# Reading exponentials from the SBUF copy, and joining two memory products in one PSUM bank, in a gated mix of two linear-attention branches

## The chip, the cores and the metric

The kernel runs on one core of one Trainium2 chip. The metric is the device time of the core in microseconds (us). Before the change it was 440.26 us, the median of six runs (439.39 to 441.11). PE is the TensorE matmul, PEld its weight load, DVE is VectorE, ACT is ScalarE, POOL is GpSimd.

## The reference, cut to what matters

Branch A is a "hedgehog" linear attention, branch B an attention in four segments with a memory carried from one segment to the next. A gate mixes their outputs. The change touches branch B alone:

```python
phi = lambda t: jnp.where(t > 0, t + 1.0, jnp.exp(t))
for s in range(4):                     # 4 segments of 512 rows; 32 heads of 20
    qs, ks, vs = q[:, :, s], k[:, :, s], v[:, :, s]
    p = _softmax(qs @ ks.T * scale + mask)
    a_dot = p @ vs
    pq = phi(qs)
    a_mem = (pq @ M) / (pq @ z + 1e-06)       # read the memory
    outs.append(g * a_mem + (1.0 - g) * a_dot)
    pk = phi(ks)
    M = M + pk.T @ vs                         # update the memory
    z = z + sum(pk)
```

## The kernel before

Branch B's loop runs over 32 groups: 4 segments times 8 groups of four heads. In each group PE makes the scores `st`, ACT turns them into `PT` by an exponential, POOL masks them, PE multiplies by the values into `nd`. Between these, PE is given "fill" work of other parts (projections of the next segment, branch A's queries, output matmuls). PE's order is fixed by hand; a scheduler orders the other engines' queues.

In this kernel every matmul writes into a tile in PSUM, from which DVE or ACT reads the result; all other tiles are in SBUF. A bank is the unit in which the kernel hands out PSUM, 512 fp32 columns on 128 partitions, and it uses eight of them. Four belong to `st` (two tiles of two banks). The other four, from the pool `psw`, are taken in turn by everything else, and that is what this case is about:

```python
psw = ctx.enter_context(tc.tile_pool(name="psw", bufs=4, space=PSUM))
ctx.enter_context(tc.manual_schedule(engines={mybir.EngineType.PE}))

def wtile(name, dt=F32):
    # ... (bf16 form cut)
    return psw.tile([P, 512], F32, name=name, tag="w")

def b_k(s, c):                                   # keys, 128 rows
    # ... (kp, pk, ek, rk: SBUF tiles)
    for hf in range(2):
        ps = wtile("kb_ps")
        mm_x(ps[:, 0:320], sc, WkB, 320 * hf, 320 * hf + 320)
        nc.vector.tensor_copy(out=kp[:, c, hf * 16:hf * 16 + 16, 0:DH],
                              in_=ps[:, 0:320].rearrange("p (h d) -> p h d", d=DH))
        if s < NSEG - 1:
            nc.scalar.activation(out=ek[:, hf * 320:hf * 320 + 320], in_=ps[:, 0:320],
                                 func=ACT.Exp)
    # ... (phi of k: rk = max(k, 0) + 1, then pk = min(rk, ek), both on DVE)

def b_q(s, g):                                   # queries of one group
    ps = wtile("qb_ps")
    # ... (five matmuls into ps)
    qT = bw.tile([P, L], BF16, name="qT", bufs=2)
    nc.vector.tensor_copy(out=qT, in_=ps)
    phiq = None
    if s > 0:
        eq = bw.tile([P, L], BF16, name="eq", bufs=1)
        nc.scalar.activation(out=eq, in_=ps, func=ACT.Exp)
        rq = bw.tile([P, L], BF16, name="rq")
        nc.vector.tensor_scalar(out=rq, in0=qT, scalar1=0.0, scalar2=1.0,
                                op0=ALU.max, op1=ALU.add)
        phiq = bw.tile([P, L], BF16, name="phiq", bufs=3)
        nc.vector.tensor_tensor(out=phiq, in0=rq, in1=eq, op=ALU.min)
    return qT, phiq

def b_mem(s, g, phiq):
    tm = None
    if s > 0:                                    # read the memory
        am = wtile("am_ps")
        for j in range(4):
            nc.tensor.matmul(am[:, j * 84:(j + 1) * 84], lhsT=phiq[:, j * P:(j + 1) * P],
                             rhs=Mbd[:, g].rearrange("p i e -> p (i e)"), start=True, stop=True)
        tm = b_norm(am, s, g, Cm, "m")           # DVE: rm = 1/den, rm *= Cm, tm = num * rm
    if s < NSEG - 1:                             # update the memory
        mz = wtile("mz_ps")
        # ... (four matmuls accumulate phi(k)^T v in mz[:, 0:84])
        # ... (DVE: Msb = mz + Msb, then Mbd = Msb * mask)
    return tm

for k in range(NG):                              # NG = 32
    # ...
    for t, cs in enumerate(((0,), (1, 3), (2,))):
        b_qk(qT, kT, PT, cs)                     # st, then PT
        if t == 0 and k + 1 < NG:
            nq = b_q(*divmod(k + 1, G))          # next group's queries
        if t == 1 and k + 1 < NG:
            nxt = (nq, b_kT(*divmod(k + 1, G)))
        if prev is not None:
            # ... t == 0: b_mem of the last group; t == 1, 2: b_pv of the last group into nd
        while fill and fill[0][0] < k + SHARE[t]:
            fill.pop(0)[1]()
```

The softmax here doesn't subtract the row's maximum and nothing guards it: scores larger than these inputs give would overflow.

## Time and profile before

| | before |
|---|---|
| device time, median | 440.26 us |
| span in the profile | 437.4 us |
| loop over the groups (101 to 412 us): PE, ACT, DVE busy | 258, 217, 185 of 311 us |
| PE waits on the q exponential `eq` | 9.6 us, 12 times |
| mean granted TensorE clock | 0.941 |

The first lines are of the page of the kernel before: busy time of each engine with its share of the span, and the chain of work that ended last, by engine. The line after them is the view by stretches for the loop (busy time and number of instructions of each engine, then granted clock, DMA share, GB/s).

```profile
PE 365.7 (84%) x4289; PEld 236.0 (54%) x4289; DVE 261.4 (60%) x680; ACT 274.8 (63%) x515; POOL 211.1 (48%) x365
...
PE 51%; ACT 19%; DVE 15%; POOL 9%; issue 4%; DMA 2%; POOLq 0%; SPq 0%; DVEq 0%; ACTq 0%
...
101.00:412.00 311.00, 257.88 (x3116) 153.83 (x3114) 185.40 (x539) 217.29 (x366) 141.76 (x251) 0.94 0.02 7
```

No engine is full. PE holds half of the chain, and the order of its matmuls is fixed (the same 4289 in the same order in the traces of before and of `qk_again`), so while one matmul waits for a bank PE stands. The view of waits for PE in the kernel before (who waited for whom: us in total, times, longest) shows for what:

```profile
PE st L428 <- ACT PT L434: 13.0, 25, 1.4
PE num_ps L518 <- DVE ts L538: 5.9, 3, 3.7
PE num_ps L518 <- ACT eq L401: 5.1, 5, 1.0
...
PE otp L551 <- ACT eq L401: 1.8, 2, 0.9
...
PE kb_ps L231 <- ACT eq L401: 1.0, 2, 0.5
...
PE kT_ps L412 <- ACT eq L401: 0.9, 2, 0.6
...
PE vb_ps L231 <- ACT eq L401: 0.8, 1, 0.8
```

Matmuls that have nothing to do with `eq` (branch A's `num_ps`, output transposes, next keys) wait for it, because they were given the bank that `eq` was still reading. One such wait, from the timeline of the kernel before (start, us, engine, instruction, in brackets the idle time before it and its releaser):

```profile
201.86 0.69 DVE L397 CAST qT<-qb_ps 128x512 bf16<-128x512 f32 x1 [1.33 <-PE qb_ps L393]
...
201.95 0.34 PE L518 MATMUL num_ps<-KVZ,Eq 128*128 128x132 bf16 x3
...
202.64 0.61 ACT L401 ACTIVATE eq<-qb_ps 128x512 bf16<-128x512 f32 x1
...
203.30 0.33 PE L518 MATMUL num_ps<-KVZ,Eq 128*128 128x132 bf16 x3 [1.01 <-ACT eq L401]
```

The DVE copy ends at 202.55, ACT's exponential of the same bank starts only then and ends at 203.25, and the second half of the `num_ps` matmuls waits 1.01 us for it.

Durations that the change rests on, from the groups by shape (count, busy us, mean ns, idle before):

```profile
L397 DVE CAST qT<-qb_ps 128x512 bf16<-128x512 f32 x32 | 22.1, 691 | 46.1 <-PE qb_ps L393 46.0
...
L401 ACT ACTIVATE eq<-qb_ps 128x512 bf16<-128x512 f32 x24 | 14.4, 602 | 4.9 <-DVE qT L397 2.7 <-DVE rq L403 1.5
...
L372 ACT ACTIVATE ek<-kb_ps 128x320 bf16<-128x320 f32 x24 | 10.3, 439 | 13.3 <-DVE kpad_150 L369 11.0 <-DVE kpad_156 L369 2.1
```

### The profile page before, as it was taken

The page shows a single profiled execution, that of the slowest core. Times are in us where ns is not written, and L with a number is a line of the kernel's source. Part 1 is how long each engine was busy: PE and PEld are TensorE (multiplying, and loading weights), DVE is VectorE, ACT ScalarE, POOL GpSimd, SP SyncE. Part 2 cuts the span into 40 slices and gives each one's busy share as a digit, 9 for nine tenths or more (in the row PEclk, how much of TensorE's full clock was granted, in tenths as well). Part 3 has the DMA queues.
Part 4 walks back from the last instruction along what each step waited for, and adds up shares of the span by engine and source line. Part 5 has one row for each costly group of instructions (what it writes and reads, how often), then busy time and mean ns, then how long its engine had stood idle before and what let it go on. Part 6 is the DMA issues. An engine that isn't in the chain of part 4 may idle for free.

```text
span 437.4 us, 10502 instructions
## 1 busy us (share of the span) xinstructions
PE 365.7 (84%) x4289; PEld 236.0 (54%) x4289; DVE 261.4 (60%) x680; ACT 274.8 (63%) x515; POOL 211.1 (48%) x365
## 2 busy tenths in 40 slices
PE   1999999797888687888988888898887788787686
PEld 1677877674444343455555555565554454445465
DVE  5378666787357453677665557665666556555431
ACT  1576666525887466676875777586675886765502
POOL 9037877860355434544453434554345555444520
PEclk9999999999999796899998999999999998988569
DMA  8960000000000000000000000000000000000001
GB/s 257 363 193 32 5 1 1 0 1 1 2 1 1 2 1 0 1 2 2 16 16 1 16 2 16 1 16 6 13 17 1 16 1 16 17 2 15 11 16 51
DMA packets 10610, 12.49 MB, mean 29 GB/s; under 512 B 1347, under 2 KB 10563, under 8 KB 10563
## 3 DMA queue, kind: packets, MB, share of 16 engines
q1 hardware_dynamic: 10563, 11.83, 8.2%
q8 instruction: 33, 0.54, 0.5%
q14 instruction: 14, 0.11, 0.1%
HBM read 9.21 MB, written 2.62 MB: 27 GB/s over the span
## 4 chain that ended last, share of the span: by engine, by line
PE 51%; ACT 19%; DVE 15%; POOL 9%; issue 4%; DMA 2%; POOLq 0%; SPq 0%; DVEq 0%; ACTq 0%
ACT PT L434 12%; PE o_ps L565 10%; PE pq_ps L500 6%; PE qb_ps L393 6%; PE st L428 4%; PE va_ps L231 4%; PE nd_ps L448 4%; PE vb_ps L231 4%; POOL PT L438 3%; PE kb_ps L231 3%; PE ka_ps L231 3%; DVE ts L538 2%; PE otp L551 2%; ACT eq L401 2%; DVE qT L397 2%
## 5 line engine op out<-in xcount | busy, mean ns | idle before, releaser
L434 ACT ACTIVATE PT<-st 128x1024 bf16<-128x1024 f32 (+1 forms) x192 | 158.7, 885 | 20.6 <-PE st L428 18.5
L438 POOL TENSOR_SCALAR_AFFINE_SELECT PT<-PT 128x512 bf16<-128x512 bf16 x128 | 80.9, 644 | 113.0 <-ACT PT L434 97.1
L231 PEld LDWEIGHTS <-xT 128*128 128x128 bf16 x640 | 61.0, 99 | 31.2 <-issue 6.4
L428 PE MATMUL st<-qT,kT 32*128 32x128 bf16 (+3 forms) x512 | 44.6, 312 | 15.1 <-ACT PT L434 13.0
L397 DVE CAST qT<-qb_ps 128x512 bf16<-128x512 f32 x32 | 22.1, 691 | 46.1 <-PE qb_ps L393 46.0
L448 PEld LDWEIGHTS <-PT 128*128 128x128 bf16 x1280 | 38.4, 97 | 10.7 <-POOL rr L529 3.9
L393 PE MATMUL qb_ps<-xT,WqB 128*128 128x512 bf16 x160 | 43.1, 403 | 1.0 <-DVE ts L538 0.8
L543 POOL TENSOR_TENSOR oA<-ts 128x360 bf16<-128x360 f32 (+1 forms) x32 | 27.6, 862 | 31.1 <-DVE ts L538 27.5
L500 PE MATMUL pq_ps<-xT,WqA 128*128 128x512 bf16 x120 | 33.7, 417 | 6.7 <-DVE ts L538 3.1
L569 ACT CAST osb<-o_ps 128x320 bf16<-128x320 f32 x32 | 13.6, 426 | 39.6 <-PE o_ps L565 39.4
L428 PEld LDWEIGHTS <-kT 32*128 32x128 bf16 x512 | 14.0, 92 | 42.3 <-issue 37.0
L503 ACT ACTIVATE Eq<-pq_ps 128x512 bf16<-128x512 f32 x24 | 14.3, 597 | 27.9 <-PE pq_ps L500 27.7
L518 PE MATMUL num_ps<-KVZ,Eq 128*128 128x132 bf16 (+1 forms) x192 | 18.5, 220 | 15.2 <-DVE ts L538 5.9
L538 DVE TENSOR_TENSOR ts<-num_ps,cs 128x360 f32<-128x360 f32 (+1 forms) x64 | 28.2, 483 | 1.9 <-DVE cs L533 0.2
L231 PE MATMUL vb_ps<-WvB,xT 128*128 128x320 bf16 x160 | 25.0, 301 | 3.8 <-DVE ts L538 2.3
L241 ACT CAST vA<-va_ps 128x320 bf16<-128x320 f32 x32 | 13.6, 426 | 23.0 <-PE va_ps L231 23.0
L251 ACT ACTIVATE Ek<-ka_ps 128x320 bf16<-128x320 f32 x64 | 23.0, 439 | 5.5 <-PE ka_ps L231 4.9
L231 PE MATMUL kb_ps<-WkB,xT 128*128 128x320 bf16 x160 | 25.5, 306 | 1.1 <-ACT eq L401 1.0
L231 PE MATMUL va_ps<-WvA,xT 128*128 128x320 bf16 (+1 forms) x160 | 25.8, 310 | 0.0
L531 DVE RECIPROCAL rr<-rr 128x18 f32<-128x18 f32 (+1 forms) x32 | 8.1, 253 | 29.3 <-POOL rr L529 29.2
L393 PEld LDWEIGHTS <-WqB 128*128 128x128 bf16 x160 | 13.7, 100 | 21.0 <-issue 9.9
L231 PE MATMUL ka_ps<-WkA,xT 128*128 128x320 bf16 x160 | 24.5, 299 | 0.4 <-DVE xT L213 0.2
(252 smaller groups left out, 751.7 us busy)
## 6 DMA issues: line engine op xcount, KB each, us to landing
out_dram<-osb SPq DMA_DIRECT2D x16, 160.0 KB, 1.8
WvA<-in_A_wqkv_dram SPq DMA_DIRECT2D x1, 800.0 KB, 5.2
wnat_k<-in_A_wqkv_dram SPq DMA_DIRECT2D x1, 800.0 KB, 6.9
wnat_q<-in_A_wqkv_dram SPq DMA_DIRECT2D x1, 800.0 KB, 11.1
WkB<-in_B_wk_dram SPq DMA_DIRECT2D x1, 800.0 KB
WvB<-in_B_wv_dram SPq DMA_DIRECT2D x1, 800.0 KB, 11.3
wq_st<-in_B_wq_dram SPq DMA_DIRECT2D x5, 160.0 KB, 7.7
WoA<-in_A_wo_dram SPq DMA_DIRECT2D x1, 800.0 KB, 10.5
```

What stands on the lines that cost most here:

```text
L231: nc.tensor.matmul(ps, lhsT=xT[:, c, sc * P:(sc + 1) * P], rhs=W[:, c, lo:hi], start=(c == 0), stop=(c == KC - 1))
L251: nc.scalar.activation(out=Ek[:, sgn, 320 * hf:320 * hf + 320], in_=ps[:, 0:320], func=ACT.Exp, scale=1.0 if sgn == 0 else -1.0)
L393: nc.tensor.matmul(ps, lhsT=WqB[:, c, 4 * g:4 * g + 4, :], rhs=xT[:, c, s * L:(s + 1) * L], start=(c == 0), stop=(c == KC - 1))
L397: nc.vector.tensor_copy(out=qT, in_=ps)
L428: nc.tensor.matmul(st2[i // 2][:, i % 2, o:o + n], lhsT=kT[r:r + 32, c * P:(c + 1) * P], rhs=qT[r:r + 32, c * P:L], start=True, stop=True, ...
L434: nc.scalar.activation(out=PT[:, 2 * pr:2 * pr + 2, base:base + w], in_=st2[pr][:, :, 0:w], func=ACT.Exp, scale=SCALE_B)
L438: nc.gpsimd.affine_select(out=view, in_=view, pattern=[[0, 4], [1, P]], compare_op=ALU.is_ge, fill=0.0, base=0, channel_multiplier=-1)
L448: nc.tensor.matmul(nd[:, j * 84 + i * V1:j * 84 + (i + 1) * V1], lhsT=PT[:, i, o:o + P], rhs=vb[:, c, 4 * g + i, :], start=(j == 0 and i = ...
L500: nc.tensor.matmul(ps, lhsT=WqA[:, c, g * 120:g * 120 + P], rhs=xT[:, c, s * L:(s + 1) * L], start=(c == 0), stop=(c == KC - 1))
L538: nc.vector.tensor_tensor(out=ts[:, sgn, 0:nh, :], in0=pss[sgn][:, :, 0:DH], in1=cs[:, sgn, 0:nh, None].to_broadcast([P, nh, DH]), op=ALU. ...
L543: nc.gpsimd.tensor_tensor(out=segs[s].oA[:, qc, h0 * DH:(h0 + nh) * DH].rearrange("p (h d) -> p h d", d=DH), in0=ts[:, 0, 0:nh, :], in1=ts ...
L565: nc.tensor.matmul(ps[:, 0:320], lhsT=segs[s].oT[qc, X][:, k5 * P:(k5 + 1) * P], rhs=Wo[:, k5, hf * 320:hf * 320 + 320], start=(n == 0), s ...
```

## The change

The intent is to shorten the time for which banks of the pool of four are held. The two exponentials `ek` and `eq` read the SBUF copies that DVE makes anyway, so the banks of local k and q come free when DVE is done. And `am` (memory read) and `mz` (memory update) go into one bank, which takes a bank 16 times less (8 groups in each of segments 1 and 2, where both exist).

```diff
@@ b_k
-            if s < NSEG - 1:
-                nc.scalar.activation(out=ek[:, hf * 320:hf * 320 + 320], in_=ps[:, 0:320],
-                                     func=ACT.Exp)
         if s < NSEG - 1:
+            nc.scalar.activation(out=ek.rearrange("p (h d) -> p h d", d=DH), in_=kp[:, c, :, 0:DH],
+                                 func=ACT.Exp)
@@ b_q
-            nc.scalar.activation(out=eq, in_=ps, func=ACT.Exp)
+            nc.scalar.activation(out=eq, in_=qT, func=ACT.Exp)
@@ b_mem
+        am = wtile("am_ps")
         if s > 0:
-            am = wtile("am_ps")
             for j in range(4):
                 nc.tensor.matmul(am[:, j * 84:(j + 1) * 84], lhsT=phiq[:, j * P:(j + 1) * P],
-                                 rhs=Mbd[:, g].rearrange("p i e -> p (i e)"), start=True, stop=True)
+                                 rhs=Mbd[:, g].rearrange("p i e -> p (i e)"), start=(j == 0),
+                                 stop=True, skip_group_check=True)
+        if s < NSEG - 1:
+            mz = am[:, 336:420]
+            for c in range(4):
+                nc.tensor.matmul(mz, lhsT=phik2[s % 2][:, c, 4 * g:4 * g + 4, :],
+                                 rhs=vB2[s % 2][:, c, 4 * g:4 * g + 4, :],
+                                 start=(c == 0 and s == 0), stop=(c == 3),
+                                 skip_group_check=True)
+        if s > 0:
             tm = b_norm(am, s, g, Cm, "m")
         if s < NSEG - 1:
-            mz = wtile("mz_ps")
-            for c in range(4):
-                ... (the same matmuls into mz[:, 0:84])
-            nc.vector.tensor_tensor(out=Msb[:, g], in0=mz[:, 0:84].rearrange(...),
+            nc.vector.tensor_tensor(out=Msb[:, g], in0=mz.rearrange(...),
                                     in1=Msb[:, g], op=ALU.add)
```

With two results in one bank only the first matmul carries `start`, the flag that begins a new sum. The Trainium skill (PSUM — Partial Sum Buffer, The four PSUM rules) gives this as one of two idioms for several accumulation groups in one bank: later groups find their bits cleared and overwrite.

More of the change, by code (lines that the diff above doesn't have):

```diff
@@ L455, in b_mem @@
         tm = None
+        am = wtile("am_ps")
         if s > 0:
-            am = wtile("am_ps")
             for j in range(4):
                 nc.tensor.matmul(am[:, j * 84:(j + 1) * 84], lhsT=phiq[:, j * P:(j + 1) * P],
-                                 rhs=Mbd[:, g].rearrange("p i e -> p (i e)"), start=True, stop=True)
+                                 rhs=Mbd[:, g].rearrange("p i e -> p (i e)"), start=(j == 0),
[8 more added lines that the diff above has]
+        if s > 0:
             tm = b_norm(am, s, g, Cm, "m")
         if s < NSEG - 1:
-            mz = wtile("mz_ps")
-            for c in range(4):
-                nc.tensor.matmul(mz[:, 0:84], lhsT=phik2[s % 2][:, c, 4 * g:4 * g + 4, :],
-                                 rhs=vB2[s % 2][:, c, 4 * g:4 * g + 4, :],
-                                 start=(c == 0), stop=(c == 3))
-            nc.vector.tensor_tensor(out=Msb[:, g], in0=mz[:, 0:84].rearrange("p (i e) -> p i e", e=V1),
+            nc.vector.tensor_tensor(out=Msb[:, g], in0=mz.rearrange("p (i e) -> p i e", e=V1),
                                     in1=Msb[:, g], op=ALU.add)
```

## The prediction

> **What bounds the kernel now.** The span is 437.4 us (440.26 us timed). The table of busy time shows PE 84%, ACT 63%, DVE 60%. By stretches, in the loop over 32 head groups (101 to 412 us) PE is busy 258 of 311 us, ACT 217, DVE 185: no engine is full. PE issues in program order, so a matmul waiting for a PSUM bank stops everything behind it. The chain of waits is PE 51%, ACT 19% (12% the PT exponentials), DVE 15%.
>
> The view of waits names what PE waited for in the loop. ACT PT before st (13.0 us) and DVE ts (about 17 us) are untouched by the change. The exponential eq costs 5.1 (num_ps), 1.8 (otp), 1.0 (kb_ps), 0.9 (kT_ps), 0.8 (vb_ps): 9.6 us in 12 waits; ek 0.8 us; tm and Msb 2.6 us.
>
> **Why eq holds a bank.** Both DVE and ACT read the q bank. The Trainium skill (PSUM — Partial Sum Buffer, Terms) says two engines may not access one bank and quadrant at once, reads included; the trace agrees: eq never starts before the qT copy (691 ns) is over, and in the timeline ends 0.74 us after it on average (24 cases, 0.63 to 1.21). So reading the SBUF copy costs no start time, and frees the bank 0.74 us earlier.
>
> **What moves.**
> - q: 24 banks free 0.74 us earlier. Of the twelve waits at most 8.9 us (12 x 0.74) goes. The next release (ts, PT) often lies close behind, so I expect 5 us.
> - k: twelve pairs of 320-wide exponentials (2 x 437 ns) become one of 640. ScalarE: Activation LUTs (What ACT_TABLE_LOAD costs) gives 186 ns + 0.833 per element; the trace's 597 ns for 512 and 1024 ns for 1024 roughly fit. Estimate 0.72 us against 0.87: 1.9 us less ACT, mostly hidden. Banks come free 0.44 us or more earlier; about 1 us.
> - SBUF instead of PSUM source: I assume eq stays within 0.05 us of 597 ns.
> - Memory: in segments 1 and 2 (16 groups) one of four rotating banks is taken less. Against this, the norm waits for the mz matmuls (0.31 us in the timeline), and Msb now stands after tm and phiq in DVE's order, so the bank is held some 0.5 us longer than am alone. Neutral: 1 us gained to 2 us lost.
>
> **How much reaches the end.** About 6 us of PE waiting goes, all in the loop. Where PE gets ahead, st will wait for PT instead (1 to 3 us more). Net gain about 5 us, 1.1%.
>
> **Predicted: 435.3 us, range 429.5 to 440.0.** Faster by over 2%: 0.15; within 2%: 0.82; slower by over 2%: 0.03.
>
> **What would show it.** Right: PE's waits on eq and ek vanish, mostly not replaced; PE's busy time unchanged, its idle time in the loop down from 53 to about 48 us; ek 12 times near 0.72 us, eq near 0.6; stretches before 101 us within 1 us. Wrong: the waits reappear under ts, qT or Msb at the same places; or eq and ek are much slower from SBUF.
>
> **What would make it wrong.** Msb or tm in the shared bank becoming a PE wait of several us; the rotation shifting so that a long-held bank (num_ps, held till ts) meets an urgent matmul; or the removed waits being worth more than their sum because ACT's exponentials start earlier in each iteration.

## The result, and the profile after

| | before | after |
|---|---|---|
| device time, median | 439.39 us (40 runs) | 437.75 us (20 runs) |
| lowest to highest | 437.0 to 441.55 | 434.6 to 443.51 |
| ratio, fast runs | 1 | 0.9944 (0.992 to 0.9967) |
| PE waits on eq and ek | 10.4 us | 0 |
| PE waits on Msb and tm | 2.6 us | 8.1 us |

A ratio is the mean time of one kernel's fast runs over that of the other's fast runs in the same rounds, so it is not quite the ratio of the medians. Four of the new kernel's 21 executions are marked slow because they lie over 1.5% above its fastest. On a single core this is no second die; the spread goes with the granted clock, as shown below. Over all timed runs, slow ones kept in, the means are 438.17 and 439.53 us, a ratio of 0.997.

The profiled execution of the new kernel took 441.08 us at clock 0.930, in the upper part of its own spread. Its busy times, chain and loop stretch:

```profile
PE 371.8 (85%) x4289; PEld 236.0 (54%) x4289; DVE 259.2 (59%) x680; ACT 273.0 (62%) x503; POOL 212.0 (48%) x365
...
PE 55%; DVE 16%; ACT 15%; POOL 8%; issue 4%; DMA 2%; POOLq 0%; SPq 0%; DVEq 0%; ACTq 0%
...
101.00:412.00 311.00, 262.75 (x3079) 153.49 (x3078) 181.80 (x532) 215.10 (x357) 141.39 (x249) 0.92 0.02 7
```

PE's work is the same, but it is busy 6 us longer than before, at a lower clock. The view of PE's waits of the new kernel has no line with `eq` or `ek` left, and three with `Msb`:

```profile
PE st L427 <- ACT PT L433: 13.8, 25, 1.6
PE num_ps L521 <- DVE ts L541: 6.5, 3, 3.7
...
PE nd_ps L447 <- DVE Msb L471: 3.3, 3, 1.8
...
PE num_ps L521 <- DVE Msb L471: 1.4, 1, 1.4
...
PE vb_ps L231 <- DVE Msb L471: 0.8, 1, 0.8
```

The exponentials cost what was assumed, within 0.03 us (groups by shape of the new kernel): 634 ns from SBUF against 602 from PSUM for `eq`, and one `ek` of 736 in place of two of 439.

```profile
L400 ACT ACTIVATE eq<-qT 128x512 bf16<-128x512 bf16 x24 | 15.2, 634 | 2.7 <-DVE qT L396 2.0 <-DVE rq L402 0.4
...
L372 ACT ACTIVATE ek<-kpad_150 128x640 bf16<-128x640 bf16 x8 | 5.9, 736 | 11.3 <-DVE kpad_150 L369 11.3
```

The largest new wait, in the timeline of the new kernel:

```profile
279.88 0.25 DVE L480 RECIPROCAL rm<-am_ps 128x16 f32<-128x16 f32 x1
...
280.21 0.17 DVE L481 TENSOR_TENSOR rm<-rm,Cm 128x16 f32<-128x16 f32 x1
...
281.43 0.24 DVE L534 RECIPROCAL rr<-rr 128x14 f32<-128x14 f32 x1 [1.05 <-POOL rr L532]
281.59 0.43 DVE L484 TENSOR_TENSOR tm<-am_ps,rm 128x320 f32<-128x320 f32 x1
281.93 0.41 DVE L405 TENSOR_TENSOR phiq<-rq,eq 128x512 bf16<-128x512 bf16 x1
282.26 0.24 DVE L471 TENSOR_TENSOR Msb<-am_ps,Msb 128x84 f32<-128x84 f32 x1
...
282.65 0.53 PE L447 MATMUL nd_ps<-vB_152,PT 128*128 128x21 bf16 x14 [1.78 <-DVE Msb L471]
```

`nd` was given the shared bank. `Msb`, the last reader of that bank, stands in DVE's queue behind `tm` and `phiq`, and `tm` stands behind `rr`, a step of branch A for which DVE waits 1.05 us on POOL. In the kernel before, `mz` had a bank of its own, and `Msb` came right after the second `rm` and ahead of `phiq` and `tm`, in all sixteen groups with both parts. One of them, from the timeline of the kernel before:

```profile
202.79 0.17 DVE L478 TENSOR_TENSOR rm<-rm,Cm 128x16 f32<-128x16 f32 x1
...
202.88 0.24 DVE L468 TENSOR_TENSOR Msb<-mz_ps,Msb 128x84 f32<-128x84 f32 x1
203.28 0.45 DVE L406 TENSOR_TENSOR phiq<-rq,eq 128x512 bf16<-128x512 bf16 x1 [0.17 <-ACT eq L401]
```

The order of DVE's queue is the scheduler's; it came out differently with the shared bank.

The same place by stretches of 1.7 us (columns as above; the first of the last three figures is the granted clock):

```profile
278.70:280.40 1.70, 1.65 (x25) 0.95 (x23) 1.10 (x4) 1.70 (x5) 0.18 (x1) 1.00 0.00 0
280.40:282.10 1.70, 0.46 (x8) 0.23 (x4) 0.67 (x3) 1.70 (x3) 0.92 (x3) 1.00 0.00 0
282.10:283.80 1.70, 1.15 (x27) 0.95 (x28) 1.70 (x7) 0.50 (x1) 0.79 (x2) 0.65 0.00 0
283.80:285.50 1.70, 1.70 (x8) 1.01 (x7) 0.59 (x2) 0.00 (x0) 1.22 (x2) 0.50 0.04 10
285.50:287.20 1.70, 1.58 (x19) 1.00 (x18) 0.89 (x2) 0.32 (x2) 0.00 (x0) 0.85 0.00 0
287.20:288.90 1.70, 1.70 (x30) 1.28 (x26) 0.84 (x4) 1.15 (x3) 0.95 (x3) 1.00 0.00 0
```

After PE's gap the clock is halved for 3.4 us (twice the sum of the missing shares 0.35, 0.50 and 0.15, times 1.7 us). The Trainium skill (TensorE: Matmul & The Clock Gate, Part 1) says that the clock is set to half or full from PE's activity in free-running windows of about 3.4 us. The stretches in these traces agree: the change's profile has thirteen at half speed, each 3.4 us or a multiple (the last is cut off by the end of the kernel), and in the 3.4 us before each PE was busy 71% or less. Not every such gap is followed by one: at the same place in `mem_only` (below) PE stands 1.46 us, and the clock stays at 1.00 for the 4.7 us that follow. And one program meets them differently: of the change's two profiled executions one has a half-speed stretch at 86 us, before the loop, the other none before 108 us. So a wait of PE may cost more than its length, depending on where it falls, and one program's runs differ in time and in mean clock together: the new kernel's from 434.6 us at 0.944 to 443.5 us at 0.922.

### The profile page after: what moved, and what is told of

Same layout as the page of the kernel before. It is cut to its first block, busy times and chain, and to the rows that moved or that the text cites. A ratio compares the mean times of both kernels' runs of the same rounds, so it can differ in the third digit from the quotient of the medians.

```text
span 439.4 us, 10479 instructions
## 1 busy us (share of the span) xinstructions
PE 371.8 (85%) x4289; PEld 236.0 (54%) x4289; DVE 259.2 (59%) x680; ACT 273.0 (62%) x503; POOL 212.0 (48%) x365
## 4 chain that ended last, share of the span: by engine, by line
PE 55%; DVE 16%; ACT 15%; POOL 8%; issue 4%; DMA 2%; POOLq 0%; SPq 0%; DVEq 0%; ACTq 0%
ACT PT L433 10%; PE o_ps L568 10%; PE qb_ps L392 7%; PE pq_ps L503 6%; PE vb_ps L231 5%; PE st L427 5%; PE va_ps L231 4%; PE kb_ps L231 4%; PE nd_ps L447 4%; PE ka_ps L231 3%; POOL PT L437 3%; DVE qT L396 2%; DVE ts L541 2%; PE otp L554 1%; ACT Eq L506 1%
## 5 line engine op out<-in xcount | busy, mean ns | idle before, releaser
L427 PE MATMUL st<-qT,kT 32*128 32x128 bf16 (+3 forms) x512 | 47.0, 317 | 16.1 <-ACT PT L433 13.8
L503 PE MATMUL pq_ps<-xT,WqA 128*128 128x512 bf16 x120 | 35.2, 431 | 6.9 <-DVE ts L541 4.2
L231 PE MATMUL vb_ps<-WvB,xT 128*128 128x320 bf16 x160 | 27.9, 325 | 3.0 <-DVE td L484 0.9
L494 POOL TENSOR_TENSOR oB<-td,tm 128x320 bf16<-128x320 f32 x24 | 20.9, 869 | 12.0 <-DVE td L484 11.5
L447 PE MATMUL nd_ps<-vB_158,PT 128*128 128x21 bf16 x640 | 21.2, 173 | 5.7 <-DVE tm L484 2.0
## 6 DMA issues: line engine op xcount, KB each, us to landing
WoA<-in_A_wo_dram SPq DMA_DIRECT2D x1, 800.0 KB, 10.4
```

What stands on the lines that cost most here:

```text
L231: nc.tensor.matmul(ps, lhsT=xT[:, c, sc * P:(sc + 1) * P], rhs=W[:, c, lo:hi], start=(c == 0), stop=(c == KC - 1))
L427: nc.tensor.matmul(st2[i // 2][:, i % 2, o:o + n], lhsT=kT[r:r + 32, c * P:(c + 1) * P], rhs=qT[r:r + 32, c * P:L], start=True, stop=True, ...
L447: nc.tensor.matmul(nd[:, j * 84 + i * V1:j * 84 + (i + 1) * V1], lhsT=PT[:, i, o:o + P], rhs=vb[:, c, 4 * g + i, :], start=(j == 0 and i = ...
L503: nc.tensor.matmul(ps, lhsT=WqA[:, c, g * 120:g * 120 + P], rhs=xT[:, c, s * L:(s + 1) * L], start=(c == 0), stop=(c == KC - 1))
```

## The experiments

Theory W: the gain is the earlier release of the q banks, and the shared memory bank gives part of it back by a late release. Theory N: the removed waits were worth little, because PE waits for something else instead, and the memory part is neutral. Theory C: the clock eats the gain. All kernels gave correct results. Intervals are 95%.

| kernel | parts | ratio, fast runs | mean clock, all runs | PE waits us: eq + ek | tm | Msb |
|---|---|---|---|---|---|---|
| before | – | 1 | 0.941 | 10.4 | 2.1 | 0.5 |
| the change | q, k, memory | 0.9944 (all runs: 0.997) | 0.936 | 0 | 2.6 | 5.5 |
| qk | q, k | 0.9829 | 0.949 | 0 | 2.6 | 1.2 |
| qk_again | q, k | 0.9879 (all runs: 0.986) | 0.945 | 0 | 3.0 | 1.1 |
| q_only | q | 0.9853 | 0.943 | 0.5 | 2.6 | 1.1 |
| k_only | k | 0.994 (all runs: 1.001) | 0.946 | 9.5 | 2.1 | 0.5 |
| mem_only | memory | 0.9963 | 0.934 | 5.0 | 1.7 | 2.1 |
| q_hold | q, bank held by ACT | 1.0058 | 0.936 | 0.8, and 9.1 on hd | 1.2 | 2.1 |
| after_late | all, phiq later on DVE | 0.9943 | 0.941 | 0 | 2.6 | 2.8 |
| after_again | all | 0.9969 (all runs: 1.001) | 0.932 | 0 | 3.0 | 5.5 |
| after_prio | all, DVE's order mended | 0.9884 | 0.946 | 0 | 7.1 | 0 |
| after_prio2 | all, DVE's order mended | 0.9917 | 0.943 | 0 | 7.1 | 0 |
| qk_prio | q, k, DVE's order as in after_prio | 0.9894 | 0.949 | 0 | 3.8 | 0 |

The waits are sums over the listed waits of PE from 100 us on, in the one profiled execution; these three columns are not all of PE's waits (see the clock section). The clock of "before" is the mean of the 33 runs made beside these experiments.

### qk: the change without its memory part

The diff is the first two parts of the change's diff; `b_mem` stays as before.

> The change without its memory part: eq and ek from the SBUF copies, am and mz in two banks as before. Theory W (waits): the local part removes PE's 10 us of waits on eq and ek, the shared memory bank gives back about 6 us as new waits on Msb; so this beats the change: 433 to 435 us, ratio to before 0.984 to 0.990, PE waits on eq, ek and Msb together under 1 us. Theory N (the memory part is neutral and the removed waits were cheap, PE waiting for PT or ts instead): same as the change, ratio 0.993 to 0.996. Theory C (the granted clock eats the gain): ratio near 0.994 with a mean clock lower than before's 0.94 by 0.01, although the waits are gone.

Measured: 430.80 us median against 439.24, ratio 0.9829 (0.9785 to 0.9872). Theory W holds for the local part, with a gain somewhat above its upper end; N and C fall for it: without the memory part there is three times the gain of the change, and the clock is higher, not lower. For the shared bank C is not ruled out (see the clock section). The waits on `eq` and `ek` are gone; 1.2 us of waits on `Msb` and 2.6 us of short waits on the copy `qT` stand in their place, so "under 1 us" for `Msb` was slightly too low. From the view of PE's waits of qk:

```profile
PE num_ps L517 <- DVE qT L396: 1.9, 6, 0.3
...
PE kT_ps L411 <- DVE Msb L467: 0.5, 2, 0.2
PE num_ps L517 <- DVE Msb L467: 0.5, 1, 0.5
...
PE vb_ps L231 <- DVE Msb L467: 0.2, 1, 0.2
```

### q_only: only eq from the copy

```diff
-            nc.scalar.activation(out=eq, in_=ps, func=ACT.Exp)
+            nc.scalar.activation(out=eq, in_=qT, func=ACT.Exp)
```

> Only eq reads the SBUF copy. Theory W: most of the gain is here, ratio 0.986 to 0.992 (eq held the bank 0.74 us in 12 observed waits of 9.6 us in all); PE waits on eq gone, on ek still about 0.8 us. Theory N: ratio 0.994 to 0.998. In both eq takes 630 ns, as in the change.

Measured: 432.38 us, ratio 0.9853 (0.9805 to 0.99), a little beyond what was expected. This one line carries nearly the whole gain of the local part.

### mem_only: only the shared memory bank

The diff is the third part of the change's diff.

> Only am and mz share a bank; eq and ek read PSUM. Theory W: slower than before by 2 to 4 us, ratio 1.004 to 1.010, with PE waits on Msb of 4 to 7 us. Theory N: ratio 0.998 to 1.002.

Measured: 437.41 us, ratio 0.9963 (0.9923 to 1.0003). Theory W expected it slower, by 2 to 4 us; it is not. On its own the memory part is neutral or slightly good. The waits of mem_only say why: the ones on `eq` fall from 9.6 to 4.2 us, although `eq` still reads PSUM, and those on `Msb` rise by 1.6 us. A further wait of 1.46 us, at the place of the change's longest, is put down to `cs`, the step of DVE after `Msb`; `nd` starts there 0.15 us after the end of `Msb`, as in the change, so it is probably the same late release.

```profile
PE kT_ps L412 <- ACT eq L401: 2.0, 7, 0.6
...
PE num_ps L522 <- DVE Msb L472: 1.1, 2, 0.7
...
PE nd_ps L448 <- DVE cs L537: 1.5, 1, 1.5
...
PE nd_ps L448 <- DVE Msb L472: 1.0, 2, 0.6
...
PE vb_ps L231 <- ACT eq L401: 0.8, 1, 0.8
...
PE num_ps L522 <- ACT eq L401: 0.8, 1, 0.8
```

So the memory part does what it is for; the likely reason is that, with 16 takings fewer, a q bank is wanted again later, when `eq` has more often ended. But this is the same waiting that the q part removes. Once the q banks come free early there is less left for the memory part to save (waits on `qT`, `td` and `kT`: 8.0 us in qk_again, 4.1 in the change), and its late release stays. The mean clock of mem_only is low (0.934); why is not settled. At a common clock the fit below gives it 435.1 us, 4 us less than before.

### after_late: phiq after the memory reads

```diff
-            phiq = bw.tile([P, L], BF16, name="phiq", bufs=3)
-            nc.vector.tensor_tensor(out=phiq, in0=rq, in1=eq, op=ALU.min)
+            phiq = (rq, eq)
# ... and in the loop, after b_mem and b_pv of step t:
+            if t == 0 and k + 1 < NG:
+                nq = b_phi(nq)      # makes phiq there
```

> The whole change, and phiq (DVE, 421 ns, which waits for eq) is given to DVE after the memory reads, so Msb no longer stands behind phiq and the shared bank comes free at least 0.4 us sooner. PE's matmuls and their order are the same. Theory W: about half of the new waits on Msb goes (5 us of PE's waits in the change, to 2 or 3), ratio 0.986 to 0.992. Theory N: same as the change, 0.993 to 0.996.

Measured: 435.57 us, ratio 0.9943 (0.9898 to 0.9989). The waits on `Msb` fell from 5.5 to 2.8 us as expected, the time did not follow clearly: it lies with the change's 0.9944. `phiq` in front of `Msb` is thus not enough as a cause; the largest gap before `nd`, 1.78 us in the change, was still 1.45 us. The timeline of after_late shows what else stands in the way: `rr`, with DVE's 1.05 us of waiting on POOL, still stands in front of `tm`.

```profile
276.25 0.24 DVE L541 RECIPROCAL rr<-rr 128x14 f32<-128x14 f32 x1 [1.05 <-POOL rr L539]
276.41 0.43 DVE L491 TENSOR_TENSOR tm<-am_ps,rm 128x320 f32<-128x320 f32 x1
276.75 0.23 DVE L478 TENSOR_TENSOR Msb<-am_ps,Msb 128x84 f32<-128x84 f32 x1
```

### after_again: the change once more

> The change itself, on the same chip and in the same rounds as the next three. Ratio 0.993 to 0.996 if what was measured first holds; about 0.994 is also the sum of the parts if the memory part gives back over half of what the local part gains.

Measured: 438.96 us, ratio 0.9969 (0.9924 to 1.0014), two of six runs slow, just above the range expected. It agrees with the first result within its interval. The two largest waits on `Msb` are again 1.8 and 1.4 us, at the same two places; these waits belong to the program, not to one run.

### after_prio and after_prio2: the shared bank, with DVE's order mended

```diff
-        if s > 0:
-            tm = b_norm(am, s, g, Cm, "m")
+        with tc.high_priority(offset=100):
+            if s < NSEG - 1:
+                nc.vector.tensor_tensor(out=Msb[:, g], in0=mz.rearrange(...),
+                                        in1=Msb[:, g], op=ALU.add)
+            if s > 0:
+                tm = b_norm(am, s, g, Cm, "m")
         if s < NSEG - 1:
-            nc.vector.tensor_tensor(out=Msb[:, g], in0=mz.rearrange(...),
-                                    in1=Msb[:, g], op=ALU.add)
             nc.vector.tensor_tensor(out=Mbd[:, g], ...)
```

> The whole change, am and mz still in one bank, but DVE is made to take Msb, rm and tm of the shared bank ahead of phiq and of the reciprocal rr, for which DVE sat 1.05 us in front of tm in the change. PE's order is the same. Theory W2 (the cost of the shared bank is its late release in DVE's order: Msb behind phiq, tm behind rr): the waits on Msb and tm fall from 7.7 us to under 3 us and the ratio comes to that of the local part alone, 0.980 to 0.986. Rival (sharing itself costs, the norm waits for eight matmuls in place of four, and fewer tiles shift the rotation): ratio 0.990 to 0.996 though the order is mended.

Measured: 433.38 us, ratio 0.9884 (0.9849 to 0.992). The expectation on waits failed: those on `Msb` vanish, but those on `tm`, now the bank's last reader, grow from 2.6 to 7.1 us, so the sum only falls from 8.1 to 7.1. From PE's waits in the second run of it:

```profile
PE nd_ps L447 <- DVE tm L486: 5.5, 6, 1.2
```

What did go is the long gaps: none of these waits is longer than 1.2 us, against 1.8 and 1.4 before, and the mean clock is 0.946 and 0.943 against the change's 0.936 and 0.932. The ratio falls between the two theories.

> The change with DVE's order mended, again, now in the same rounds as qk and qk_prio. If the late release was the whole cost of the shared bank, it comes out within 0.3% of qk_prio. If it stays 0.4% or more behind, the rest lies in sharing: rm and tm wait for eight matmuls, and am's bank, now held for both parts, is the next one that nd needs (waits on tm before nd of 5.5 us against 2.4).

Measured: 435.37 us, ratio 0.9917 (0.9884 to 0.995), beside qk_prio's 0.9894: 0.23% apart, inside the 0.3% named. Set against qk_again in the same rounds (0.9879) it is 0.4% behind. With intervals of about 0.4% on each side neither difference is secure.

### qk_prio: the control

```diff
-            tm = b_norm(am, s, g, Cm, "m")
+            with tc.high_priority(offset=100):
+                tm = b_norm(am, s, g, Cm, "m")
# ... and the same around Msb; two banks as before
```

> The local part alone, am and mz in two banks, with DVE taking Msb and the memory norm early as in after_prio. Control for that run. Theory W2 (only the order of release on DVE mattered): same as qk, as its two banks were not released late; the waits on tm stay near 2.4 us; ratio 0.979 to 0.987. A better ratio than 0.978 would say that the early order helps by itself, and then that after_prio's gain over the change says less about the shared bank.

Measured: 434.37 us, ratio 0.9894 (0.9868 to 0.992), a little worse than expected; the waits on `tm` are 3.8 us and not near 2.4. The early order does not help by itself; it may even cost a few tenths of a per cent. So what after_prio gained over the change is not a general benefit of that order.

### q_hold: give the gain back

```diff
-            nc.scalar.activation(out=eq, in_=ps, func=ACT.Exp)
+            nc.scalar.activation(out=eq, in_=qT, func=ACT.Exp)
+            hd = bw.tile([P, 2], BF16, name="hd", bufs=1)
+            nc.scalar.copy(out=hd, in_=ps[:, 0:2])
```

> q alone, eq reads the SBUF copy, and right after eq ACT copies two columns from the q bank to a scratch tile: the bank is held by ACT as before, everything else is as in q_only. Theory W (the gain of q_only is the bank's earlier release): the gain is gone or turned round, ratio 0.997 to 1.010, PE waits of 8 to 14 us on the small copy; ACT has 24 x about 0.2 us = 5 us more to do. Rival (the gain comes from the order or from reading SBUF): ratio stays at 0.985 to 0.992.

Measured: 440.02 us, ratio 1.0058 (1.001 to 1.0105). `eq` reads SBUF as in q_only, yet the whole gain is gone, with 9.1 us of waits on the small copy, in the places where `eq` stood:

```profile
PE num_ps L520 <- ACT hd L403: 4.9, 5, 1.4
...
PE otp L553 <- ACT hd L403: 1.9, 2, 1.0
```

The copy takes 143 ns, 3.4 us of ACT's time in all 24, of which no more than a part can be on the chain; the difference between q_only and q_hold is 2%. The gain of the q part is the release of the bank, not the source of the read.

### k_only: only ek from the copy

The diff is the first part of the change's diff.

> Only ek reads the SBUF copy, one exponential of 640 in place of two of 320. PE waited 0.8 us on ek before. Every theory: small, ratio 0.994 to 1.001; with q_only (0.9853) times this one near the 0.9829 of both together if the parts add up.

Measured: 439.66 us, ratio 0.994 (0.9904 to 0.9976) over its three fast runs; the other three, at 442 us and clock 0.938, are marked slow, and all six together give 1.001. With q_only alone at 0.9853 and both at 0.9829 and 0.9879, the k part is not distinguishable from nothing.

### qk_again

> The local part alone once more, in other rounds: ratio 0.980 to 0.987 if the first measurement (0.9829) holds; the best so far, faster than the change by over 1%.

Measured: 433.02 us, ratio 0.9879 (0.9835 to 0.9922), just outside the weak end, 0.987, of what was expected; and the lead on the change is 0.65 to 0.9%, not the over 1% expected. The two measurements of this kernel average 0.985. With q_only, which differs from it by the k part alone, it is the best version here.

### What the runs say of the clock

The 120 runs of all kernels above, fitted with one time per kernel and one common slope, give 3.5 us less time for each 0.01 of mean clock, with a scatter of 0.8 us. At a common clock of 0.94 the fit gives 439.1 us for before, 437.0 and 436.7 for the change, 435.8 and 436.2 for after_prio, and 434.4 and 434.5 for qk. So of the 7 us between the change and qk, all runs kept, about 2.5 us stays at a common clock and some 4.5 us goes with a clock that is lower by 0.013. This split is a correlation: a long gap may lower the clock and a low clock lengthens the run, and no experiment set the clock by itself.

By the waits of the table two kernels do not fit (k_only at 441.4 us, qk_prio at 437.2). By all of PE's waits over 0.15 us, 100 us onward, they do: 56.8 us in k_only and 51.1 in qk_prio, against 53.9 before and 48.1 in q_only; over the thirteen profiled executions these sums go with the times at a common clock (correlation 0.91). But by these sums the change is no worse than qk: 48.6 us against 48.3 in qk_again, both from traces with all 4289 matmuls, since 4.4 us more on `Msb` stand against 3.9 us less on `qT`, `td` and `kT`. (after_again has 51.6 us. Eight of the thirteen traces, after_again's, k_only's and q_only's among them, lack 32 of the 4289 matmuls, which can swell the gaps.) What is larger in the change is PE's busy time, 371.8 us at clock 0.930 against 360.3 at 0.955. A slow clock can also cover waits, so whether the shared bank costs time by waiting or by the clock is not settled.

## Why the prediction was right or wrong

- **Total.** Predicted 435.3 us, range 429.5 to 440.0; measured 437.75. The range held, and "within 2%" was right. The expected gain of 5 us came out near half: 0.56% of about 439 us is 2.5 us. That it came this near is in part luck: the local part gained some 6.6 us (0.985) and not 5, and the memory part lost some 4 us and not about nothing.
- **q release.** Right, and shown. The waits on `eq` vanished, q_only alone gained 1.5% (0.0147 of 439 us, 6.5 us, against the 5 predicted), and q_hold took it back.
- **k exponentials.** The durations were right (0.737 us against 0.72). The gain of 1 us was not found; k_only is unclear.
- **Source in SBUF.** `eq` became 0.03 us slower, inside the 0.05 assumed.
- **Memory, "neutral: 1 us gained to 2 us lost".** In time this is the term that was mis-sized. By itself it is indeed neutral (0.9963), but next to the local part it costs about 0.9% (0.9944 over the 0.985 of qk), some 4 us. Two things were missed. First, the two parts of the change remove the same waits on `eq`, so their gains cannot be added. Secondly, the late release was seen ("some 0.5 us longer") but taken as an average. In the profile there are worst cases: twice DVE's queue put the last read of the shared bank so late that PE stood 1.8 and 1.4 us. One of these was behind a wait of DVE on POOL for branch A, which the prediction named only in general ("Msb or tm in the shared bank becoming a PE wait of several us"). That these gaps are what costs the 4 us is not shown: summed over all waits the term was near what was predicted (48.6 us in the change, 48.3 in qk_again).
- **Clock.** The prediction took a wait of PE at its length, and PE's busy time as unchanged. Its test on idle time came out: in the loop stretch PE's idle time fell from 53 to 48 us, as it said. But PE was busy there 262.75 us and not 257.88, with fewer matmuls done (3079 against 3116), at clock 0.92 against 0.94, in an execution from the upper part of the spread. So there the idle time went as predicted, and busy time at a lower clock took the gain. The trace shows half-speed stretches of 3.4 us after gaps, so waits that remain long may cost more than their length. How much of the 4 us this makes is only correlated.
- **What stays open.** after_prio wins back some of the loss (0.9884 and 0.9917 against the change's 0.9944 and 0.9969), which fits the late release as its cause, although all its waits together (48.1 us in the complete trace) are hardly fewer than the change's 48.6. How much of the rest comes from sharing itself, from the waits on `tm` or from the clock, the intervals do not tell.

## What to carry to other kernels

When several engines read a PSUM bank, look in the waits of PE for its last reader: moving that read to a copy in SBUF that exists anyway frees the bank at little cost to the reader (0.03 us per exponential here), and here one line was worth 1.5%. Two remedies for the same bank pressure need not add up, as these two did not; measure each alone and both together. Joining two results in one bank makes the bank as late as the later reader, at the worst place of that engine's queue, so read the order of that queue and not only the number of banks. And before a named wait is called the cost, sum all the waits and look at the clock: here the new waits on `Msb` were made up elsewhere.

## What the Trainium skill lacked or had wrong

- ScalarE: Activation LUTs (What ACT_TABLE_LOAD costs) gives one formula, 186 ns + 0.833 ns per element, without naming the source, which makes 612 ns for 512 elements and 719 for 640. Here 512 elements took 597 ns (median) from PSUM in fp32 and 630 ns from SBUF in bf16, and 640 from SBUF took 737: this formula is 15 ns too high from PSUM and 18 ns too low from SBUF. (Other pages of the skill do keep the two sources apart, so the difference itself is not lacking.)
- TensorE: Matmul & The Clock Gate (Part 1) has the clock fall to half after at least one idle window of about 3.4 us. Here a stretch of 3.4 us at half speed followed a gap of 1.78 us, in which PE was still busy 0.46 of 1.70 us. The length of the stretch agrees.
- The same page (A second HAM failure mode: psum-queue depth-cycling) describes a clock that swings because PE pauses between groups while it goes round its PSUM banks, which may be what these traces show, but gives no size for it. Here runs of one unchanged program spread from 434.6 us at clock 0.944 to 443.5 us at 0.922, which is 2%, nearly twice the gain of 1.1% that was predicted.
- PSUM — Partial Sum Buffer tells how to put several groups in one bank and does not say what it costs: here the bank was held until the last reader of both, with 5.5 us of waits of PE on it, up to 1.8 us each, against 0.5 us before. No page gives a size for it.
